# Cross-attention over states and a PReLU feed-forward on one Trainium2 core: batch 1's state scores with tokens in partitions, and the table of steps in another order

## Chip, cores and metric

The kernel runs on one core of one Trainium2 chip. The metric is the device time of one launch in microseconds; the median of the runs shown is 208.47 us (207.69 to 208.61, three runs). Profile times below are microseconds from the start of one profiled execution's span.

## What is computed

`x` holds 8 batches of 8 heads, 512 tokens and 64 values; `state` holds 32 states of 64 values for each batch and head. Tokens read states, states read tokens, and all rows go through one feed-forward layer with a PReLU:

```
scores = scale * x @ state^T             # 512 x 32 for each batch and head
xread  = softmax(scores over states) @ state
sread  = softmax(scores^T over tokens) @ x
rows   = concat(xread, sread)            # 4352 rows of 512 (8 heads x 64)
h      = rows @ w_in                     # 4352 x 2048
out    = (max(h,0) + alpha * min(h,0)) @ w_out
```

## The kernel before

The work is cut into named steps, and one table of text, `ORDER` (lines 17 to 136), lists them; the loop at line 830 executes the table word by word. A word such as `F.0.3.7` is the step's name with its arguments, often with a PSUM bank (0 to 7) or an engine (`a` ScalarE, `v` VectorE, `p` GpSimd) at its end. Each engine works through its own instructions in the order of the table, so the table is each engine's queue; what waits for what follows from the data and from the eight banks. The names that matter here:

- `wi`, `wo`, `lx`, `lst` (lines 252, 258, 199, 246): loads of a quarter of w_in or w_out, of one batch of x, of the states of batches 2 to 7. All are issued from GpSimd's queue. Only four batches of x fit, so a late `lx` also waits for the batch whose place it takes.
- `xt`, `xo`, `xo2` (lines 332, 344, 347): transposing x of batches 0 and 1 on TensorE and copying the result to `xT`. Later batches are transposed by DMA from SyncE's queue (SP), `xd` (line 326).
- Softmax over states, one of two ways. By transposition: `sc` (line 353) makes the scores with states in partitions, `sb` (463) transposes them in 32 x 32 blocks on VectorE, `smax` (475) takes maxima on VectorE, `ssh` (480) subtracts them on GpSimd, `sexp` (486) takes the exponential on ScalarE. By TensorE: `dd` (396) copies the states into a block-diagonal tile, `sd` (403) makes the scores with tokens in partitions, `hm` (419) takes maxima on VectorE, `hs` (422) subtracts them with one more matmul, `he` (432) takes the exponential on ScalarE straight from PSUM. Both ways end alike: `ssum` (490), `snorm` (495, GpSimd), `wb` (503, VectorE), which gives the weights `aT`. A batch is done by TensorE if the table has an `sd` word for it (line 376). Before, this is batch 0 alone.
- Softmax over tokens: it always uses `sc`; then `tm` (512, VectorE), `tms` and `te` (518, 521, ScalarE), `tsum` (535), a DMA transposition `tt` (539, SP), and the products and copies `rd`, `rn`, `rt`, `rdo` (546 to 576).
- The first matrix product is folded: `m` (585) multiplies the states by a quarter of w_in, `mo` (600) casts the result to f16 on ScalarE or VectorE, and `f` or `F` (637, 614), the "first products", multiply it with `aT`. `N` (649, ScalarE) rectifies, `G` (654, VectorE) finishes the PReLU.
- The second product: batch 0 plainly, `S` (671), 32 words of two matmuls of 512 columns. Batches 1 to 7, and the state rows as an eighth group, combine blocks into seven products where eight would be needed: `W` (733, GpSimd) forms sums of w_out's blocks, `A` (756, GpSimd or VectorE) sums of hidden blocks, `P` (767) the products, four matmuls of 256 columns a word, `C` and `D` (802, 807) the copies and sums to the output rows, `st` (721) the store from SP. There are four output buffers.
- `Z` (268) issues dummy matmuls in TensorE's idle head: its last argument counts pieces of 128 columns, up to four in one matmul.

Of the kernel before, what the change touches and what calls it, by code (L numbers as in the profile page):

```python
# [22 lines left out]
mo.2.0.a.1.2 mo.2.0.a.0 Z.4.5 xt.1.1.0.5 xt.1.0.0.5 xo2.1.0.v xt.1.1.1.6 xt.1.0.1.6 xo2.1.1.v
f.0.2.0.4 f.0.2.1 N.0.2.0 G.0.2 F.0.3.7 N.0.3.1 G.0.3 m.3.0.1.2 mo.3.0.a.1.3 mo.3.0.a.0 Z.5.4
m.0.1.0.3 mo.0.1.a.1.4 wo.3 mo.0.1.a.0 lx.2 sc.1.2.5.6 tm.1 f.0.0.0.4 f.0.0.1 N.0.0.2 sb.1 f.0.1.0.2
f.0.1.1 N.0.1.3 G.0.1 tms.1 m.4.0.7.1 mo.4.0.a.0.5 te.1.0 te.1.1 m.0.2.0.3 mo.0.2.v.0.6 m.1.1.7.2
mo.1.1.a.1.7 mo.4.0.a.1 mo.1.1.a.0 mo.0.2.v.1 smax.1 lx.3 ssh.p.1 W.1.0.p W.1.1.p G.0.0 F.0.5.0
F.0.7.5 m.1.3.6.3 mo.1.3.a.0.8 mo.1.3.v.1 F.0.4.2 N.0.4.0 G.0.4 N.0.7.1 G.0.7 N.0.5.3 F.0.10.1
F.0.6.7 tsum.0 F.0.8.6 N.0.8.2 G.0.8 G.0.5 m.0.3.4.3 N.0.10.0 G.0.10 mo.0.3.a.0.9 mo.0.3.a.1
S.0.1.0.2 S.0.1.1 S.0.2.0.5 S.0.2.1 m.2.1.6.4 mo.2.1.v.0.10 sexp.1 ssum.1 snorm.p.1 N.0.6.1 G.0.6  # L30
m.1.2.0.3 mo.1.2.a.1.11 mo.1.2.a.0 S.0.2.2 F.0.9.1 S.0.1.2 F.0.13.6 N.0.9.2 G.0.9 N.0.13.3 G.0.13
F.0.11.3 N.0.11.0 G.0.11 S.0.0.0.0 S.0.0.1 S.0.0.2 wb.1 F.0.15.7 F.0.12.1 S.0.1.3 N.0.15.1 G.0.15
F.0.14.6 N.0.14.2 G.0.14 S.0.2.3 S.0.1.4 S.0.0.3 N.0.12.3 G.0.12 mo.2.1.a.1 F.1.5.3 N.1.5.0 G.1.5
F.1.12.7 N.1.12.1 G.1.12 F.1.0.4 N.1.0.2 G.1.0 F.1.1.6 F.1.3.1 N.1.3.3 G.1.3 S.0.2.4 F.1.4.3 N.1.4.0
G.1.4 F.1.8.7 N.1.8.1 G.1.8 S.0.1.5 S.0.2.5 N.1.1.2 G.1.1 F.1.2.4 N.1.2.3 G.1.2 F.1.15.1 N.1.15.0
G.1.15 S.0.1.6 S.0.1.7 O.0.1.a.0 F.1.10.3 N.1.10.1 G.1.10 S.0.2.6 S.0.0.4 xd.2 sc.2.2.6.7 sb.2 tm.2
m.4.2.2.4 mo.4.2.a.0.12 smax.2 S.0.2.7 O.0.2.a.1 mo.4.2.a.1 S.0.3.0.1 F.1.9.3 N.1.9.2 G.1.9 tsum.1
F.1.11.2 N.1.11.3 G.1.11 W.0.0.p W.2.1.p W.0.1.p W.2.0.p W.3.1.p W.3.0.p A.1.0.3.0.p.0 A.1.1.3.0.p.1
tms.2 te.2.1 F.1.6.5 N.1.6.0 G.1.6 S.0.3.1 S.0.3.2 F.1.7.4 S.0.0.5 te.2.0 N.1.7.1 G.1.7 S.0.0.6
S.0.0.7 O.0.0.a.2 tt.0 tt.1 rd.0.3 rd.1.6 rn.1 A.1.1.1.0.v.0 A.1.0.3.1.v.0 m.2.3.7.2 mo.2.3.a.0.13  # L40
mo.2.3.a.1 xd.3 st.0.2 st.0.1 tt.2 S.0.3.3 F.1.13.5 ssh.p.2 sexp.2 N.1.13.2 m.3.1.0.4 mo.3.1.a.1.1
mo.3.1.a.0 A.1.1.2.0.p.0 rn.0 sc.3.2.6.7 tm.3 tms.3 lx.4 A.1.0.1.0.p.1 ssum.2 snorm.p.2 S.0.3.4
P.1.1.1.0.2 F.1.14.3 P.1.1.1.1 G.1.13 N.1.14.3 G.1.14 A.1.1.1.1.p.0 S.0.3.5 S.0.3.6 P.1.0.2.0.4
P.1.0.1.0.0 S.0.3.7 te.3.0 te.3.1 tt.3 sb.3 P.1.1.2.0.5 P.1.1.2.1 C.1.1.1.a.3 D.1.1.0 P.1.0.1.1
O.0.3.a.1 st.0.3 st.0.0 tsum.2 wb.2 m.2.2.3.1 mo.2.2.a.1.4 mo.2.2.a.0 m.3.2.6.7 mo.3.2.a.0.6 rd.2.5
lx.5 xd.4 A.1.1.2.1.p.0 P.1.0.2.1 mo.3.2.a.1 rt.0.1 rdo.0.a rn.2 smax.3 P.1.1.6.0 A.1.0.2.0.v.1
A.1.0.4.0.p.0 F.2.7.3 N.2.7.0 G.2.7 F.2.1.5 N.2.1.1 G.2.1 C.1.0.1.a.0 D.1.0.0 F.2.8.6 N.2.8.2 G.2.8
F.2.2.7 F.2.3.1 N.2.2.3 N.2.3.0 G.2.2 P.1.0.6.0 F.2.5.3 N.2.5.1 P.1.1.6.1 F.2.0.5 N.2.0.2 G.2.5
G.2.3 P.1.0.5.0.4 C.1.1.2.a F.2.11.6 N.2.11.3 G.2.11 G.2.0 A.1.0.1.1.p.1 P.1.0.5.1 F.2.9.7 P.1.1.7.0
F.2.10.3 N.2.10.1 xd.5 G.2.10 F.2.4.1 N.2.9.0 G.2.9 F.2.14.6 N.2.4.3 G.2.4 N.2.14.2 G.2.14  # L50
A.1.1.3.1.p.1 A.1.0.2.1.p.1 P.1.0.6.1 C.1.0.2.a P.1.1.7.1 ssh.p.3 sexp.3 ssum.3 P.1.1.5.0.5 F.2.13.3
rt.2.7 rdo.2.a P.1.0.7.0 C.1.1.3.a.1 P.1.0.7.1 C.1.0.3.a.2 D.1.0.1 F.2.12.1 N.2.12.1 F.2.6.6
P.1.1.5.1 G.2.12 N.2.6.0 F.2.15.7 N.2.15.3 A.1.0.4.1.p.0 G.2.6 G.2.15 N.2.13.2 G.2.13 P.1.0.4.0
P.1.0.4.1 A.2.0.1.0.p.1 C.1.0.4.a A.1.1.4.0.p.1 P.1.0.3.0 A.2.1.3.0.p.1 P.1.0.3.1 D.1.0.2 st.1.0
D.1.1.1 P.1.1.4.0 P.1.1.4.1 C.1.1.4.a st.1.3 tsum.3 rd.3.6 rn.3 sc.4.2.0.1 snorm.p.3 wb.3 m.3.3.7.3
m.4.1.4.2 mo.4.1.a.0.9 mo.3.3.a.1.0 mo.3.3.a.0 A.1.1.4.1.p.1 A.2.0.2.0.p.1 P.1.1.3.0 mo.4.1.a.1
A.2.1.1.0.v.0 A.2.0.4.0.v.0 P.2.0.1.0.6 P.2.0.1.1 P.2.0.2.0.4 C.2.0.1.a.0 F.3.5.3 N.3.5.1
A.2.0.1.1.v.1 A.2.0.2.1.p.1 F.3.1.7 N.3.1.0 tm.4 tms.4 P.2.0.6.0 P.2.0.2.1 D.2.0.0 G.3.5 F.3.3.2
N.3.3.3 G.3.3 st.1.1 P.1.1.3.1 D.1.1.2 G.3.1 st.1.2 F.3.12.4 N.3.12.2 P.2.0.6.1 C.2.0.2.a G.3.12
F.3.2.3 N.3.2.1 G.3.2 F.3.10.2 N.3.10.3 A.2.0.3.0.p.0 P.2.0.7.0 F.3.8.5 N.3.8.0 G.3.8 G.3.10 te.4.0  # L60
P.2.1.1.0.7 P.2.1.1.1 C.2.1.1.a.1 te.4.1 P.2.1.2.0.4 P.2.1.2.1 D.2.1.0 sb.4 A.2.0.3.1.p.1 F.3.9.3
P.2.0.7.1 A.2.1.1.1.p.0 N.3.9.2 sc.5.2.4.5 tm.5 A.2.1.2.0.p.0 F.3.0.2 N.3.0.1 C.2.0.3.a.2 G.3.0 lx.6
A.2.1.2.1.p.0 A.2.1.4.1.p.0 A.2.1.3.1.p.0 A.2.1.4.0.p.1 smax.4 ssh.p.4 P.2.1.6.0 P.2.1.6.1 C.2.1.2.a
F.3.13.0 N.3.13.0 tms.5 G.3.9 G.3.13 te.5.1 F.3.7.1 P.2.0.4.0 P.2.0.4.1 C.2.0.4.a te.5.0 tt.5 sb.5
P.2.1.7.0 F.3.11.2 P.2.1.7.1 N.3.7.3 C.2.1.3.a.3 P.2.0.5.0.6 P.2.0.5.1 D.2.0.1 A.3.1.3.0.p.0
A.2.0.4.1.p.1 lx.7 N.3.11.1 G.3.11 G.3.7 A.3.0.3.0.p.1 m.7.2.3.0 mo.7.2.a.1.11 mo.7.2.a.0 P.2.1.4.0
P.2.1.4.1 rt.3.5 P.2.1.5.0.4 P.2.1.5.1 sexp.4 C.2.1.4.a D.2.1.1 ssum.4 snorm.p.4 rdo.3.a F.3.6.0
N.3.6.2 G.3.6 m.5.0.2.3 mo.5.0.a.0.7 m.5.2.1.7 mo.5.2.a.0.8 P.2.1.3.0 F.3.4.5 N.3.4.0 G.3.4
mo.5.2.a.1 mo.5.0.a.1 st.2.3 P.2.0.3.0 P.2.0.3.1 F.3.15.2 N.3.15.1 D.2.0.2 st.2.0 P.2.1.3.1 D.2.1.2
st.2.1 m.4.3.0.1 mo.4.3.a.0.2 m.6.0.7.5 mo.6.0.a.0.4 m.5.1.3.6 mo.5.1.a.0.10 F.3.14.4 N.3.14.3  # L70
A.3.1.1.0.p.1 P.3.1.1.0.0 P.3.0.1.0.7 P.3.0.1.1 P.3.1.1.1 mo.5.1.a.1 mo.4.3.a.1 mo.6.0.a.1 smax.5
wb.4 ssh.p.5 G.3.15 G.3.14 P.3.1.2.0.3 A.3.0.1.0.v.0 F.4.8.6 N.4.8.2 G.4.8 tsum.4 F.4.5.1 N.4.5.0
C.3.1.1.a.3 C.3.0.1.a.0 G.4.5 P.3.1.2.1 F.4.15.2 F.4.12.4 D.3.1.0 N.4.12.1 G.4.12 F.4.10.5 N.4.10.3
G.4.10 P.3.0.2.0.6 F.4.6.1 N.4.6.2 P.3.0.2.1 F.4.2.3 N.4.2.0 G.4.6 D.3.0.0 G.4.2 F.4.7.4 N.4.7.1
G.4.7 N.4.15.3 G.4.15 A.3.0.1.1.p.1 A.3.0.2.0.p.1 P.3.0.6.0 F.4.13.5 N.4.13.2 F.4.14.1 F.4.3.6
# [787 lines left out]
```

## Time and profile before

| | us |
|---|---|
| runs shown, median | 208.47 |
| the profiled execution | 207.22 |
| its span | 205.4 |
| TensorE busy | 197.1 (96%) |
| VectorE busy | 181.6 (88%) |
| GpSimd busy | 159.6 (78%) |
| ScalarE busy | 145.2 (71%) |

The profiled execution is 1.82 longer than its span. Busy time of TensorE counts each matmul with its modelled end, so neighbours overlap; where many follow each other, the time from start to start is the better measure. The TensorE clock was granted in full (1.00) in every stage.

### The profile page before, as it was taken

Reading aid. Unit: us, or ns where it says so; the run is one execution under the profiler, and the core shown is the slowest. Engines: PE = TensorE matmul, PEld = TensorE weight load, DVE = VectorE, ACT = ScalarE, POOL = GpSimd, SP = SyncE. Lnnn points to the kernel's source line nnn. Section 1 sums busy time; section 2 is a strip of 40 time slices with the busy share of each in tenths; the row PEclk is TensorE's granted clock in tenths of the full one; section 3 lists DMA queues with packets and bytes.
Section 4 is the critical chain, followed back from the end, with each engine's and each line's share of the span. In section 5 each row is a group of like instructions: output and inputs, shape, how many; then the busy total and the mean of one; then the engine's idle time right before and its main releaser. Section 6 shows DMA issues by size and latency. Waiting matters only on the chain.

```text
span 205.4 us, 5181 instructions
## 1 busy us (share of the span) xinstructions
PE 197.1 (96%) x2023; PEld 131.4 (64%) x2023; DVE 181.6 (88%) x321; ACT 145.2 (71%) x319; POOL 159.6 (78%) x136
## 2 busy tenths in 40 slices
...
GB/s 81 195 203 209 204 206 197 185 232 54 163 163 178 66 153 58 100 103 158 194 163 3 53 123 135 3 105 102 0 0 3 111 93 3 2 131 62 69 102 156
DMA packets 39257, 23.22 MB, mean 113 GB/s; under 512 B 22320, under 2 KB 35008, under 8 KB 39232
## 3 DMA queue, kind: packets, MB, share of 16 engines
...
q1 hardware_dynamic: 26496, 14.29, 28.4%
...
HBM read 17.31 MB, written 8.91 MB: 128 GB/s over the span
## 4 chain that ended last, share of the span: by engine, by line
PE 85%; DVE 5%; DMA 5%; POOL 1%; ACT 1%; issue 1%; ACTq 0%; POOLq 0%
PE ps L793 44%; PE ps L620 24%; PE ps L675 7%; DMA xg<-in_x_dram 5%; PE ps L629 3%; PE ps L590 3%; DVE gt_all L656 3%; PE ps L553 1%; ACT neg_all L652 1%; PE ps L362 1%; DVE m_all L603 1%; POOL xg L218 1%; DVE ts L466 1%; DVE nb L514 1%; DVE mx L476 1%
## 5 line engine op out<-in xcount | busy, mean ns | idle before, releaser
L656 DVE SCALAR_TENSOR_TENSOR gt_all<-neg_all,oma_sb,ps 128x512 f16<-128x512 f32 x128 | 89.3, 738 | 3.0 <-ACT neg_all L652 2.7
L652 ACT ACTIVATE neg_all<-ps 128x512 f32<-128x512 f32 (+1 forms) x144 | 77.4, 598 | 20.0 <-PE ps L620 14.4
L620 PE MATMUL ps<-aT,m_all 128*128 128x512 f16 x250 | 66.4, 379 | 0.3 <-DVE m_all L603 0.2
L765 POOL TENSOR_TENSOR hc_all<-gt_all 128x512 f16<-128x512 f16 x43 | 49.2, 1160 | 11.4 <-DVE osb_all L810 8.7
L793 PEld LDWEIGHTS <-hc_all 128*128 128x128 f16 x480 | 46.3, 98 | 14.3 <-issue 1.1
L793 PE MATMUL ps<-wc,hc_all 128*128 128x256 f16 x360 | 47.7, 273 | 0.0
L793 PEld LDWEIGHTS <-gt_all 128*128 128x128 f16 x336 | 32.6, 98 | 8.3 <-issue 0.5
L805 ACT COPY osb_all<-ps 128x256 f32<-128x256 f32 x51 | 19.1, 383 | 25.7 <-PE ps L793 22.2
L620 PEld LDWEIGHTS <-m_all 128*128 128x128 f16 x250 | 24.0, 98 | 18.0 <-issue 2.2
L603 ACT CAST m_all<-ps 128x512 f16<-128x512 f32 x58 | 31.6, 621 | 4.3 <-PE ps L590 4.3
L765 POOL TENSOR_TENSOR hc_all<-gt_all,hc_all 128x512 f16<-128x512 f16 x22 | 25.4, 1164 | 6.3 <-DVE hc_all L765 6.1
L793 PE MATMUL ps<-w_out_sb,gt_all 128*128 128x256 f16 x224 | 29.7, 273 | 0.0
L765 POOL TENSOR_TENSOR hc_all<-hc_all,gt_all 128x512 f16<-128x512 f16 x21 | 24.3, 1164 | 3.9 <-DVE hc_all L765 3.6
L810 DVE TENSOR_TENSOR osb_all<-osb_all,ps 128x256 f32<-128x256 f32 x45 | 18.0, 413 | 7.6 <-PE ps L793 4.7
L496 POOL TENSOR_TENSOR an<-ts,r 128x1024 f16<-128x1024 f32 (+1 forms) x9 | 15.5, 1725 | 6.2 <-DVE r L493 4.0
L482 POOL TENSOR_TENSOR ts<-ts,mx 128x1024 f32<-128x1024 f32 x7 | 13.4, 1918 | 5.4 <-DVE mx L476 5.4
L675 PE MATMUL ps<-w_out_sb,gt_all 128*128 128x512 f16 x64 | 16.6, 380 | 0.1
L793 PE MATMUL ps<-w_out_sb,hc_all 128*128 128x256 f16 x120 | 16.5, 273 | 0.0
L793 PE MATMUL ps<-wc,gt_all 128*128 128x256 f16 x112 | 14.7, 273 | 0.0
L590 PE MATMUL ps<-w_in_sb,stT 64*32 64x512 f16 x256 | 11.8, 383 | 1.9 <-DMA w_in_sb<-in_moe_w_in_dram 0.9
L527 ACT ACTIVATE e<-ps,nb 128x512 f16<-128x512 f32 x16 | 11.1, 705 | 0.1
L675 PEld LDWEIGHTS <-gt_all 128*128 128x128 f16 x64 | 5.9, 98 | 7.2 <-issue 1.2
...
## 6 DMA issues: line engine op xcount, KB each, us to landing
...
w_in_sb<-in_moe_w_in_dram POOLq DMA_DIRECT2D x4, 512.0 KB, 12.0
w_out_sb<-in_moe_w_out_dram POOLq DMA_DIRECT2D x4, 512.0 KB, 13.6
...
```

What stands on the lines that cost most here:

```text
L482: engine(e).tensor_tensor(ts, ts, over_blocks(cols(softmax_tile("mx", b), j, S // N)), ALU.subtract)
L496: engine(e).tensor_tensor(blocks(cols(softmax_tile("an", b), j, S)), blocks(cols(softmax_tile("ts", b), j, S)), over_blocks(cols(softmax_t ...
L590: nc.tensor.matmul(banks[N * k : N * (k + 1), (k0, k1)[g], :], st_head(b, 2 * k + g)[64 * g : 64 * g + 64, :], w_in_sb[64 * g : 64 * g + 6 ...
L603: copier(e)(ms[b, f][:, g, :], banks[:, live["mp", b, f][g], :])
L620: nc.tensor.matmul(h.rearrange("p (r t) -> p r t", r=2), ms[b, f][:, g, 128 * j : 128 * (j + 1)], weights(b, g), start=(g == 0), stop=(g = ...
L652: nc.scalar.activation(neg, h, RELU, bias=0.0, scale=-1.0)
L656: nc.vector.scalar_tensor_tensor(gts[b, f][:, j, :], negs.pop((b, jc)), oma_sb[:, jc : jc + 1], hs.pop((b, jc)), ALU.mult, ALU.add,)
L675: nc.tensor.matmul(outs[b, q], hidden(b, jc, q), w_out_sb[:, jc, :], start=(jc == 0), stop=(jc == n_jc - 1),)
L765: engine(e).tensor_tensor(t, x, y, ALU.add if s == 1 else ALU.subtract)
L793: nc.tensor.matmul(outs[b, i, bank], rows, cols, start=(p in (1, 2, 5) and jc == 0), stop=(jc == n_jc // 2 - 1), skip_group_check=True,)
L805: copier(e)(rows_at(b, q, k)[:, 256 * half : 256 * (half + 1)], outs[b, i, "x"])
L810: nc.vector.tensor_tensor(to, to, outs[b, i, bank], ALU.add)
```

## The change

Only the table changes. The code of the steps is the same, two lines further down, since the table is two lines longer: L362 before is L364 after.

```diff
-lx0.0 lx0.1 id ni.v wi.0 oma lst stc Z.7.32 stt.2 sto.a lx.1 wi.1 dd.0.0.v wi.2 Z.7.3 xt.0.0.0.6
+lx0.0 lx0.1 id ni.v wi.0 stc oma wi.1 Z.3.22 stt.7 dd.0.1.a dd.0.0.a lx.1 lst Z.3.10 xt.0.0.0.0
```

What the new table does:

- Batch 1 has `sd`, `hm`, `hs`, `he` in place of `sb`, `smax`, `ssh`, `sexp`. Its `sc` stays, for the softmax over tokens.
- `sc.0`, `sc.1` and the token softmaxes of batches 0 and 1 come after the first products have begun (`sc.1` after twelve of them); before, `sc.0` stood ahead of all.
- The transposes of batch 1 (`xt.1`) come after six first products have begun; before, they stood ahead of the first.
- The first dummies are 22 pieces where they were 32. The second half of batch 0's `hs` comes after the first `m`; before, both halves came ahead of it.
- Engines: VectorE does four `A` (28, were 32), two `mo` (4, were 6), two `xo`, one `xo2` and one `dd` fewer, and two `C` and one `rdo` more. The `A` go to GpSimd, the others to ScalarE or from it.
- Everything behind that, to the last product, is in another order too; the number of first and second products is the same.

GpSimd's queue at its head, before: the loads of w_in, of the states (`gs_all`), of batch 1 (`xg_124`), of w_out, of batches 2 and 3, with batch 0's normalisation (L496) between them.

```order
L253 DMA w_in_sb<-in_moe_w_in_dram 128x4x512
L247 DMA gs_all<-in_state_dram 128x768
L201 DMA xg_124<-in_x_dram 128x8x256
L253 DMA w_in_sb<-in_moe_w_in_dram 128x4x512 x3
L496 TENSOR_TENSOR an_298<-ts_240,r_0_242 128x512 x2
L259 DMA w_out_sb<-in_moe_w_out_dram 128x4x512 x4
L201 DMA xg_377<-in_x_dram 128x8x256
L201 DMA xg_443<-in_x_dram 128x8x256
```

The same place after the change (lines are two higher):

```order
L255 DMA w_in_sb<-in_moe_w_in_dram 128x4x512 x2
L203 DMA xg_123<-in_x_dram 128x8x256
L249 DMA gs_all<-in_state_dram 128x768
L255 DMA w_in_sb<-in_moe_w_in_dram 128x4x512
L498 TENSOR_TENSOR an_231<-ts_225,r_0_228 128x512 x2
L261 DMA w_out_sb<-in_moe_w_out_dram 128x4x512
L255 DMA w_in_sb<-in_moe_w_in_dram 128x4x512
L261 DMA w_out_sb<-in_moe_w_out_dram 128x4x512 x3
```

The second quarter of w_in moved ahead of batch 1's x, the states behind it, and the last quarter of w_in behind the first of w_out.

ScalarE's queue at its head, before: copies of the states and of xT, batch 0's exponentials over states (L433), casts of m products (L603), batch 0's exponentials over tokens (L527), rectifiers (L652).

```order
L300 COPY stT<-ps 128x512
L398 COPY gs_all<-ps 64x8x32
L345 COPY xT_134<-ps 128x4x128
L433 ACTIVATE ts_240<-ps 128x512 x2
L603 CAST m_all<-ps 128x512 x2
L519 ACTIVATE nb_237<-nb_237 128x2
L603 CAST m_all<-ps 128x512
L317 COPY stT<-ps 128x128x6
L527 ACTIVATE e_0_307,r_0_308<-ps,nb_237 128x512 x2
L603 CAST m_all<-ps 128x512 x2
L652 ACTIVATE neg_all<-ps 128x512 x2
L603 CAST m_all<-ps 128x512 x4
```

After, from batch 0's exponentials over states (now L435):

```order
L435 ACTIVATE ts_225<-ps 128x512 x2
L605 CAST m_all<-ps 128x512 x7
L654 ACTIVATE neg_all<-ps 128x512 x6
L350 COPY xT_327<-ps 128x4x256
L654 ACTIVATE neg_all<-ps 128x512 x2
L319 COPY stT<-ps 128x128x6
L605 CAST m_all<-ps 128x512 x5
L654 ACTIVATE neg_all<-ps 128x512 x3
L435 ACTIVATE ts_490<-ps 128x512
```

The exponentials over tokens left this place; seven casts stand ahead of the first rectifier, then six rectifiers in a row.

SP's queue around batch 6's transposition, before (`xT_1697` is batch 6, `xT_1777` batch 7; `e2T` are transposed exponentials over tokens):

```order
L722 DMA out_dram<-osb_all 128x512 x3
L327 DMA_TRANSPOSE xT_1697<-xg_1350 128x16x128
L541 DMA_TRANSPOSE e2T_1699<-e_4_1293 128x8x128
L722 DMA out_dram<-osb_all 128x512
L327 DMA_TRANSPOSE xT_1777<-xg_1416 128x16x128
```

After (`xT_1744` and `xT_1943`):

```order
L724 DMA out_dram<-osb_all 128x512 x5
L329 DMA_TRANSPOSE xT_1744<-xg_1552 128x16x128
L543 DMA_TRANSPOSE e2T_1766<-e_5_1594 128x8x128
L724 DMA out_dram<-osb_all 128x512
L543 DMA_TRANSPOSE e2T_1909<-e_4_1291 128x8x128
L329 DMA_TRANSPOSE xT_1943<-xg_1617 128x16x128
```

Two transposes of exponentials now stand between the two batches, and five stores ahead of batch 6. In the table batch 6's load stood ahead of batch 4's normalisation and stands behind it now.

More of the change, by code (lines that the diff above doesn't have):

```diff
@@ L23 @@
[L23 to L75, printed above, removed]
@@ new lines @@
+N.1.0.3 G.1.0 F.1.3.7 N.1.3.0 G.1.3 N.1.11.1 S.0.2.4 G.1.11 A.1.0.3.0.p.0 A.1.1.1.0.p.0 F.1.5.2
+S.0.1.7 S.0.2.5 F.1.14.4 xd.2 sc.2.2.6.7 sb.2 tm.2 smax.2 ssh.p.2 N.1.5.2 O.0.1.a.0 G.1.5 N.1.14.3
+G.1.14 F.1.15.3 N.1.15.0 S.0.2.6 S.0.2.7 O.0.2.a.1 F.1.7.5 N.1.7.1 G.1.15 G.1.7 S.0.3.5 S.0.3.6
+S.0.0.0.1 S.0.0.1 S.0.0.2 S.0.0.3 tms.2 te.2.1 A.1.0.1.0.p.1 te.2.0 A.1.0.2.0.p.0 m.4.2.2.6
+mo.4.2.a.0.12 F.1.12.7 N.1.12.2 G.1.12 F.1.13.4 N.1.13.3 G.1.13 A.1.0.1.1.p.0 sexp.2 ssum.2
+snorm.p.2 S.0.3.7 S.0.0.4 S.0.0.5 S.0.0.6 S.0.0.7 O.0.3.a.2 mo.4.2.a.1 m.3.2.5.2 mo.3.2.a.0.13
```

177 lines of the change are left out of this document (113 added, 64 removed).

## Prediction

> **What bounds the kernel now.** I read the page first, then busy time by stage, then the chain that ended last.
>
> ```profile
> PE 197.1 (96%) x2023; PEld 131.4 (64%) x2023; DVE 181.6 (88%) x321; ACT 145.2 (71%) x319; POOL 159.6 (78%) x136
> ```
>
> TensorE (PE) is busiest, VectorE (DVE) close behind. By stage (columns: busy time of PE, weight loads, DVE, ACT, POOL):
>
> ```profile
> 10.00:20.00 10.00, 8.17 (x128) 3.70 (x128) 9.46 (x15) 9.13 (x22) 6.80 (x8) 1.00 1.30 204
> 20.00:30.00 10.00, 9.20 (x72) 3.67 (x72) 9.96 (x17) 10.00 (x22) 6.08 (x3) 1.00 1.24 207
> 30.00:40.00 10.00, 10.00 (x48) 4.54 (x47) 10.00 (x15) 7.97 (x16) 9.94 (x5) 1.00 1.28 192
> ```
>
> From 10 to 30 us DVE and ScalarE (ACT) are full while PE is not; from 30 on PE is full. The chain says the same (start, length, engine, line):
>
> ```profile
> 4.76 9.53 DMA xg<-in_x_dram
> 14.34 1.07 PE ps L340 x16
> ...
> 16.51 1.41 DVE gt_all L656 x2
> ...
> 24.41 0.67 DVE gt_all L656
> 25.12 1.89 PE ps L675 x8
> ...
> 34.19 2.16 PE ps L620 x10
> ...
> 97.61 0.61 ACT neg_all L652
> ...
> 180.04 21.85 PE ps L793 x200
> ```
>
> Batch 1's load of x lands at 14.29, its transposes stand on PE ahead of the first product, DVE carries the chain from 16.51 to 25.08, and from 25.12 PE runs almost without a gap to 201.89; the last copy and store take 3.5 more. The one exception lies around 97.61:
>
> ```profile
> 99.86 0.37 ACT L805 COPY osb_all<-ps 128x256 f32<-128x256 f32 x1 [0.90 <-DMA out_dram<-osb_all]
> ```
>
> ACT waits 0.90 us for a store to free an output buffer, and products wait for ACT. So the change can gain in two places: the head, and this gap. The rest is PE's own work, which only grows.
>
> **What is added and removed.**
>
> ```profile
> 7.48 0.94 PE L409 MATMUL ps<-gs_all,xT 128*32 128x64 f16 x64
> L423 PE MATMUL ps<-gs_all 128*128 128x512 bf16 x2 | 0.8, 376 | 0.1
> L466 DVE STREAM_TRANSPOSE ts<-ps 128x1024 f32<-128x1024 f32 x7 | 8.7, 1243 | 0.0
> L476 DVE TENSOR_REDUCE mx<-ts 128x32 f32<-128x1024 f32 x7 | 8.5, 1209 | 0.0
> L420 DVE TENSOR_REDUCE gs_all<-ps 128x16 bf16<-128x512 f32 x2 | 1.3, 687 | 0.0
> L482 POOL TENSOR_TENSOR ts<-ts,mx 128x1024 f32<-128x1024 f32 x7 | 13.4, 1918 | 5.4 <-DVE mx L476 5.4
> L603 DVE CAST m_all<-ps 128x512 f16<-128x512 f32 x6 | 4.0, 682 | 0.0
> L603 ACT CAST m_all<-ps 128x512 f16<-128x512 f32 x58 | 31.6, 621 | 4.3 <-PE ps L590 4.3
> L345 DVE COPY xT<-ps 128x512 f16<-128x512 f16 x3 | 1.2, 412 | 0.4 <-PE ps L340 0.4
> L765 POOL TENSOR_TENSOR hc_all<-gt_all 128x512 f16<-128x512 f16 x43 | 49.2, 1160 | 11.4 <-DVE osb_all L810 8.7
> L765 DVE TENSOR_TENSOR hc_all<-gt_all 128x512 f16<-128x512 f16 x13 | 5.4, 426 | 0.0
> ```
>
> PE gains 64 score matmuls (0.94, of which 0.23 was a wait) and two corrections (0.38 each, 0.22 when something follows at once): **+1.1 us**. Batch 1's whole scores for the token softmax (L362) stay, so nothing leaves PE. DVE loses the transposition (1.24) and the maxima (1.21), gains two small maxima (1.37) and gives away two casts (1.36), two copies of xT (0.82) and four hidden sums (1.70); its other copies come and go and nearly cancel: about -5. ACT takes the casts (2 x 0.62) and copies, some +3 in all (an estimate: five copies more at about the length of a cast, against three fewer short ones). GpSimd (POOL) loses one subtraction (1.92) and gains four sums (4.64): +2.7. DVE, the engine of the old head chain, is relieved; ACT and POOL are loaded.
>
> **The head, walked by the queues.** The loads come one after another:
>
> ```profile
> 3.46 0.77 POOL L253 DMA_DIRECT2D w_in_sb<-in_moe_w_in_dram  x1
> DMA to landing us min/median/max: 6.6/12.0/15.3
> 13.45 3.04 POOL L259 DMA_DIRECT2D w_out_sb<-in_moe_w_out_dram  x4
> DMA to landing us min/median/max: 11.0/13.6/16.3
> ```
>
> The first quarter of w_in lands at 3.46 + 6.6 = 10.06, the first of w_out at 13.45 + 11.0 = 24.45; between them come the states and five loads of 512 KB, so some 2.7 us each. In the new order: w_in 0 at 10.1, w_in 1 at 12.7, x of batch 1 at 15.5, states 16.5, w_in 2 at 19.3, w_out 0 at 22, w_in 3 at 24.6. The second w_in is 4 us sooner, the last 2 us later.
>
> Batch 0's second correction (L423) now stands behind the first m product (L590), which waits for w_in at 10.13; so its exponential starts at 10.8 instead of 9.73, but the weights are ready at 14.2 against 14.75, since DVE is free. The first product then runs at 14.4 instead of 15.24, as no transposes of batch 1 are ahead of it. ACT now has seven casts ahead of the first rectifier. Start to start they are short:
>
> ```profile
> 21.64 2.10 ACT L603 CAST m_all<-ps 128x512 f16<-128x512 f32 x4
> 23.54 2.65 ACT L652 ACTIVATE neg_all<-ps 128x512 f32<-128x512 f32 x5
> 29.83 2.62 DVE L656 SCALAR_TENSOR_TENSOR gt_all<-neg_all,oma_sb,ps 128x512 f16<-128x512 f32 x4
> 32.37 1.24 DVE L504 STREAM_TRANSPOSE aT<-an 128x1024 f16<-128x1024 f16 x1
> ```
>
> Four casts take 23.54 - 21.64 = 1.90 (0.48 each), rectifiers alike, prelus on DVE (32.37 - 29.83)/4 = 0.64. So the first rectifier starts at 14.6, the first prelu at 15.3 (16.51 before), and the first second product (L675) at 23.0 (25.12 before). From there PE waits again: for the two exponentials of batch 1 on ACT (banks), for casts, and for the last scores of batch 0, whose banks wait for a prelu at 30.3. By hand this gives 13 second products, 16 first products and 12 m products done at 34.1. Before, the chain from 25.12 to the end of the row 34.19 (36.35) had 13, **21** and 12 done. The missing five first products take 5 x 0.432 = 2.16 (ten matmuls in the row 34.19), so equal work is done at 34.1 + 2.16 = 36.26 against 36.35: **-0.1 us**, with the added score work already paid. For a dozen semaphore hops that my walk sums at nothing I add **+0.3**. Bounds: if PE lost nothing behind 23.0, the head would be worth -1.0; at the mean 0.62 of a cast instead of 0.48, some 30 ACT operations on the path bring +1.6 or more.
>
> **The rest.** The gap at 97.61 goes: there the store stood one product ahead of the copy that needs its buffer, now ten products and a first product (5 us) ahead: **-0.5** (0 to -0.9). POOL, followed through its queue with 1.16 a sum, ends batch 1's sum A.1.0.2.1 at 55.1, and PE wants it at 54.9: **+0.2** (0 to +1.5). The third term is batch 6's transposition:
>
> ```profile
> 80.12 0.94 POOL L201 DMA_DIRECT2D xg<-in_x_dram  x1
> 92.04 1.91 POOL L496 TENSOR_TENSOR an<-ts,r 128x1024 f16<-128x1024 f32 x1
> DMA to landing us min/median/max: 5.9/5.9/5.9
> 94.63 5.66 SPq L327 DMA_TRANSPOSE xT<-xg  x1
> DMA to landing us min/median/max: 7.7/7.7/7.7
> 111.80 0.22 PE ps L362 x16
> ```
>
> The load of batch 6 was issued at 80.12, ahead of batch 4's normalisation (92.04); now it stands behind it, so it is issued at 92 to 93 and lands 5.9 later, at 98 to 99. The transposition (7.7 to landing while a load runs beside it) ends at 106 to 107. Its user, batch 6's scores, came at 111.80 with 9 us to spare; they now stand 3.9 us of PE work earlier, at some 107. So 9 us of cover shrink to about none: **+0.5** (0 to +3). SP's queue behind it holds two transposes of exponentials, a store and batch 7's transposition, whose user comes six us of PE work later.
>
> Sum: -0.1 + 0.3 - 0.5 + 0.2 + 0.5 = **+0.4 us**. The profiled execution took 207.22 with a span of 205.4, so it would become 207.6; the runs shown have a median of 208.47, 1.25 above it, so I forecast **208.9 us**. A measurement of this kernel tells about 0.5% (1.04 us) from no change.
>
> **A rule of the skill.**
>
> ```profile
> 1.32 3.60 PE L272 MATMUL ps<-gs_all 128*128 128x512 f16 x8 [1.32 <-DVE gs_all L266]
> 6.09 0.70 PE L272 MATMUL ps<-gs_all 128*128 128x512 f16 x3
> ```
>
> The first eight dummy matmuls come 0.43 apart, those at 6.09 about half of that. The Trainium skill (TensorE: Matmul & The Clock Gate, "What's actually happening") says that the array starts at half clock and is released after about one busy window of 3.4 us. The trace agrees: 3.6 us of dummies, then full speed. The new order issues 5.5 such matmuls (2.4 us) before a short gap, so by that rule release could come a window later; doubling the transposes (0.61 for eight) and scores would bring about +0.6 us on the first exponential, most of it hidden by the wait for w_in at 10.13: an estimate of +0.2, which I leave out of the sum.
>
> **The rivals.**
> Relief of DVE pays fully (chance 0.22, faster): PE loses nothing behind 23.0 (-1.0), the old gap goes (-0.5), and no transposition is late: about -1.5 to -2, 206.7. For it speaks DVE's 9.96 of 10 in the old head; against it that ACT was as full there (10.00) and gets more.
> ACT takes DVE's place (0.20, slower): 30 operations at 0.55 to 0.62 instead of 0.48 make the head +1 to +2.5 longer than I walk it; 210.4. It decides from 0.52 each on. ACT had 9.13 and 10.00 of 10 in those stages.
> The late load of batch 6 (0.18, slower): if POOL gets to it only at 95, PE, which takes its work in order, stops at batch 6's scores for 2 to 3 us, and batch 7's follow: 211. It decides once the transposition lands later than 107.
> That the change does not do what it says (no relief, since batch 1's token scores, maxima and exponentials stay) is the forecast itself: 0.40.
>
> Chances: faster by over 0.5% 0.22, within 0.40, slower 0.38. The range takes the faster rival's centre and the late load's: 206.8 to 211.2; the likeliest case alone is 207.9 to 209.5.
>
> **What would show it.** Right: first product near 14.4, first L675 matmul near 23.0 and PE gaps until 31; DVE below 9 of 10 between 10 and 30, ACT at 9 or more; load of batch 6 behind 91 us; its scores less than 2 us behind the landing. Wrong: PE without a gap from 23 on (then faster), or a PE gap of over 1 us between 104 and 110, or sums of POOL as releasers of PE (then slower).

## The result and the profile after

The changed kernel takes **219.2 us** (median of 4 runs, 217.8 to 219.5) against 208.08 for the kernel before, measured on the same chip (207.66 to 208.61): a ratio of **1.051** (95% interval 1.047 to 1.055). The forecast was 208.9 with a range that ended at 211.2. The profiled execution took 219.0 with a span of 217.2. Code lines lie two higher than before (the hidden sums were L765 and are L767; in some experiments the table is a line shorter or longer, and they are L766).

The page's busy line for PE and the granted clock in 40 slices, of the changed kernel:

```profile
PE 202.3 (93%) x2094; PEld 133.7 (62%) x2094; DVE 187.8 (86%) x314; ACT 148.7 (68%) x325; POOL 162.3 (75%) x139
...
PE   7999999999905999999998999999999999999993
...
PEclk9999999999975899999999999999999999999999
```

PE has one hole, in the slices from 59.7 to 70.6 us, and in it the clock falls: by microsecond the granted clock is 1.00 up to 62, 0.51 in the next and 0.50 from there to 72. PE's list of waits has one entry that matters:

```profile
PE ps L622 <- DVE gt_all L658: 8.4, 1, 8.4
...
PE ps L364 <- DMA xT<-xg: 0.6, 1, 0.6
```

PE waited 8.4 us for one prelu (L658). The timeline of DVE and then of POOL around it (start, length, engine, line, operation, count):

```profile
55.65 1.18 DVE L478 TENSOR_REDUCE mx<-ts 128x32 f32<-128x1024 f32 x1
56.75 0.41 DVE L812 TENSOR_TENSOR osb_all<-osb_all,ps 128x256 f32<-128x256 f32 x1
57.08 10.00 DVE L767 TENSOR_TENSOR hc_all<-gt_all 128x512 f16<-128x512 f16 x2
```

```profile
55.26 2.27 POOL L767 TENSOR_TENSOR hc_all<-gt_all 128x512 f16<-128x512 f16 x2
57.47 0.94 POOL L203 DMA_DIRECT2D xg<-in_x_dram  x1
58.43 1.17 POOL L767 TENSOR_TENSOR hc_all<-hc_all,gt_all 128x512 f16<-128x512 f16 x1
59.53 0.91 POOL L203 DMA_DIRECT2D xg<-in_x_dram  x1
60.46 1.92 POOL L484 TENSOR_TENSOR ts<-ts,mx 128x1024 f32<-128x1024 f32 x1
62.34 1.15 POOL L767 TENSOR_TENSOR hc_all<-hc_all,gt_all 128x512 f16<-128x512 f16 x1
63.44 4.64 POOL L767 TENSOR_TENSOR hc_all<-gt_all,hc_all 128x512 f16<-128x512 f16 x4
```

Two hidden sums stand on DVE there, A.1.1.3.0 and A.1.1.3.1, and take 10.00 us together. DVE's row of that line gives minimum, median and maximum in ns:

```profile
L767 DVE TENSOR_TENSOR hc_all<-gt_all x13: 382/417/9337, 57.1 to 206.3; 128x512 f16<-128x512 f16 x13
```

The median is 0.42 us; the sum that starts at 57.74 takes 9.34 (the one ahead of it 0.74). It shows as busy, so no list of waits names it: DVE seems to work for 9 us on a sum of 0.42. All that time POOL runs without a pause. What follows on PE, from its timeline:

```profile
67.79 1.86 PE L622 MATMUL ps<-aT,m_all 128*128 128x512 f16 x4 [8.43 <-DVE gt_all L658]
...
73.01 1.03 PE L622 MATMUL ps<-aT,m_all 128*128 128x512 f16 x4
```

Four first-product matmuls take 1.86 us behind the hole (first row) and 1.03 five microseconds later (last row): PE works at half clock from 67.79 to some 72.2 (in between, rows of four matmuls of 256 columns take 1.06 instead of 0.60), which costs half of that stretch, about 2.2 us. The Trainium skill (TensorE: Matmul & The Clock Gate, "What's actually happening") has the array fall back to half clock after an idle window of some 3.4 us; the trace agrees roughly here, with half clock 2.7 us behind the end of the last matmul (59.36). So 8.4 + 2.2 + 0.6 (batch 6's scores) = 11.2 us: nearly all of the 11.4 by which the profiled 219.0 misses its forecast of 207.6 starts from one sum.

### The profile page after: what moved, and what is told of

It reads as the page before. It is cut to its first block, busy times and chain, and to the rows that moved or that the text cites. A ratio compares the mean times of both kernels' runs of the same rounds, so it can differ in the third digit from the quotient of the medians.

```text
span 217.2 us, 5320 instructions
## 1 busy us (share of the span) xinstructions
PE 202.3 (93%) x2094; PEld 133.7 (62%) x2094; DVE 187.8 (86%) x314; ACT 148.7 (68%) x325; POOL 162.3 (75%) x139
## 4 chain that ended last, share of the span: by engine, by line
PE 83%; DVE 9%; DMA 3%; ACT 1%; POOL 1%; issue 1%; DVEq 0%; POOLq 0%
PE ps L795 41%; PE ps L622 23%; PE ps L677 7%; DVE hc_all L767 5%; PE ps L592 4%; PE ps L631 3%; DMA xT<-xg 3%; DVE gt_all L658 2%; PE ps L274 1%; PE ps L555 1%; PE ps L364 1%; ACT m_all L605 1%; PE ps L342 1%; POOL xg L220 1%; POOL an L498 0%
## 5 line engine op out<-in xcount | busy, mean ns | idle before, releaser
L658 DVE SCALAR_TENSOR_TENSOR gt_all<-neg_all,oma_sb,ps 128x512 f16<-128x512 f32 x128 | 88.8, 738 | 6.9 <-ACT neg_all L654 6.7
L622 PE MATMUL ps<-aT,m_all 128*128 128x512 f16 x250 | 66.7, 386 | 8.4 <-DVE gt_all L658 8.4
L767 POOL TENSOR_TENSOR hc_all<-gt_all 128x512 f16<-128x512 f16 x43 | 49.4, 1165 | 8.6 <-PE ps L795 3.9
L622 PEld LDWEIGHTS <-m_all 128*128 128x128 f16 x250 | 23.9, 99 | 28.0 <-issue 11.3
L795 PEld LDWEIGHTS <-gt_all 128*128 128x128 f16 x336 | 32.4, 98 | 8.8 <-issue 1.2
L605 ACT CAST m_all<-ps 128x512 f16<-128x512 f32 x60 | 32.3, 611 | 5.3 <-PE ps L592 5.1
L807 ACT COPY osb_all<-ps 128x256 f32<-128x256 f32 x49 | 18.3, 385 | 23.6 <-PE ps L795 21.8
L767 POOL TENSOR_TENSOR hc_all<-gt_all,hc_all 128x512 f16<-128x512 f16 x24 | 27.6, 1165 | 9.1 <-PE ps L795 6.9
L795 PE MATMUL ps<-w_out_sb,gt_all 128*128 128x256 f16 x224 | 30.4, 273 | 0.0
L767 POOL TENSOR_TENSOR hc_all<-hc_all,gt_all 128x512 f16<-128x512 f16 x22 | 25.3, 1157 | 2.7 <-DVE hc_all L767 2.3
L812 DVE TENSOR_TENSOR osb_all<-osb_all,ps 128x256 f32<-128x256 f32 x45 | 18.2, 412 | 7.8 <-PE ps L795 5.3
L677 PE MATMUL ps<-w_out_sb,gt_all 128*128 128x512 f16 x64 | 16.0, 379 | 0.0
L767 DVE TENSOR_TENSOR hc_all<-gt_all 128x512 f16<-128x512 f16 x13 | 14.4, 1126 | 0.0
L592 PE MATMUL ps<-w_in_sb,stT 64*32 64x512 f16 x256 | 12.4, 384 | 0.3 <-DMA w_in_sb<-in_moe_w_in_dram 0.2
L484 POOL TENSOR_TENSOR ts<-ts,mx 128x1024 f32<-128x1024 f32 x6 | 11.5, 1916 | 0.0
```

The costliest lines, as they stand in the source:

```text
L484: engine(e).tensor_tensor(ts, ts, over_blocks(cols(softmax_tile("mx", b), j, S // N)), ALU.subtract)
L592: nc.tensor.matmul(banks[N * k : N * (k + 1), (k0, k1)[g], :], st_head(b, 2 * k + g)[64 * g : 64 * g + 64, :], w_in_sb[64 * g : 64 * g + 6 ...
L605: copier(e)(ms[b, f][:, g, :], banks[:, live["mp", b, f][g], :])
L622: nc.tensor.matmul(h.rearrange("p (r t) -> p r t", r=2), ms[b, f][:, g, 128 * j : 128 * (j + 1)], weights(b, g), start=(g == 0), stop=(g = ...
L658: nc.vector.scalar_tensor_tensor(gts[b, f][:, j, :], negs.pop((b, jc)), oma_sb[:, jc : jc + 1], hs.pop((b, jc)), ALU.mult, ALU.add,)
L677: nc.tensor.matmul(outs[b, q], hidden(b, jc, q), w_out_sb[:, jc, :], start=(jc == 0), stop=(jc == n_jc - 1),)
```

## The experiments

The question was what holds that sum. Theory A: any unbroken run of POOL instructions. Theory B: only a sum that meets the issue of a load, with more work queued on POOL. The rival to both: the sums were waited for, or something behind them is late whatever runs them.

**Sums on POOL.** The edit to the changed kernel:

```
- A.1.1.3.0.v.1 A.1.1.3.1.v.1
+ A.1.1.3.0.p.1 A.1.1.3.1.p.1
```

> The changed kernel, with its two sums A.1.1.3.0 and A.1.1.3.1 on GpSimd instead of VectorE. Theory (VectorE shut out by GpSimd): the 9.34 us sum is gone, PE has no wait of 8 us near 60, the clock stays at 1.0, and the time falls by 9.5 to 11 us to 208.5 to 210; GpSimd's queue gets 2 x 1.16 = 2.3 us longer. Rival (the two sums were waited for, and something behind them is late whatever runs them): PE still waits over 3 us between 57 and 70, time above 213.

Measured: 213.15 us, ratio 1.023 (1.017 to 1.030). The hole is gone, so the sums on DVE made it. But the time stopped 3 us short of what was expected, and at 213.15 it even lies where the rival had it (above 213), though without the rival's wait of over 3 us. Three costs stand in this profile: POOL, lengthened by 2.3 us, is itself late; behind that wait the clock falls (four matmuls take 1.06 at 73.32); and it fell in the head too:

```profile
71.16 0.61 PE L795 MATMUL ps<-wc,hc_all 128*128 128x256 f16 x4 [2.33 <-POOL hc_all L767]
72.27 0.61 PE L795 MATMUL ps<-wc,hc_all 128*128 128x256 f16 x4 [0.50 <-POOL hc_all L767]
...
73.32 1.06 PE L795 MATMUL ps<-w_out_sb,hc_all 128*128 128x256 f16 x4
```

```profile
11.05 0.41 PE L592 MATMUL ps<-w_in_sb,stT 64*32 64x512 f16 x8 [1.71 <-DMA w_in_sb<-in_moe_w_in_dram]
...
12.39 2.42 PE L274 MATMUL ps<-gs_all 128*128 128x512 f16 x6
```

In this execution the first quarter of w_in let PE go on at 11.05 (9.71 in the profile of the changed kernel); behind the wait six dummies took 2.42 (1.31 there) and the first product ran at 16.41 (14.37). An estimate from these rows: 2.0 us in the head, 2.8 of waits for POOL and 1.7 for half clock from 73.0 to 76.4 make 6.5 us. That is about what lies between this profiled execution (214.49) and the one of the last version below (208.66, with waits of 0.67 of its own). Both falls of the clock came behind waits shorter than the window of that rule (1.71, and 2.33 with 0.50); there the measurement decides. The four runs, 211.57 to 214.49, have mean clocks of 0.997 to 0.984, the fastest the highest and the slowest the lowest.

**Loads behind the run.** The sums stay on DVE, the loads leave:

```
- lx.4 A.1.1.2.0.p.1 lx.5 smax.3 ...
+ A.1.1.2.0.p.1 smax.3 ...
- A.1.1.3.0.v.1 A.1.1.3.1.v.1 F.2.13.2
+ A.1.1.3.0.v.1 A.1.1.3.1.v.1 lx.4 lx.5 F.2.13.2
```

> The changed kernel, with the loads of batches 4 and 5 issued behind GpSimd's run of sums instead of ahead of it and inside it; the two sums stay on VectorE. Theory A (any unbroken run of GpSimd instructions shuts VectorE out): the run is 2 x 0.95 us shorter but still some 7 us, so one of the two sums takes 6.5 to 8 us, and the time is 216 to 218. Theory B (the issue of a load shuts VectorE out, and what follows is kept waiting by it): both sums take 0.4 to 1.6 us, and the time is 208.5 to 210.

Measured: 215.78 us, ratio 1.037 (1.032 to 1.042). Its time, just under the 216 to 218 of theory A and far from the 208.5 to 210 of theory B, looks like A; the profile says the opposite:

```profile
57.19 2.04 DVE L766 TENSOR_TENSOR hc_all<-gt_all 128x512 f16<-128x512 f16 x2
```

```profile
78.19 0.63 PE L363 MATMUL ps<-xT,stT 64*32 64x256 f16 x16 [4.88 <-DMA xT<-xg]
78.75 1.89 PE L621 MATMUL ps<-aT,m_all 128*128 128x512 f16 x4
```

The two sums take 2.04 us, not 10.00, in a run of POOL's sums just as long. What is slow now is batch 4's transposition, since its load was issued at 66.52: PE waits 4.88 us and then works at half clock (1.89 for four matmuls). A total alone would have picked the wrong theory.

**One sum of the kernel before moved to DVE** (A.3.0.2.1, `.p.1` to `.v.1`):

> The kernel before, with one sum, A.3.0.2.1, moved from GpSimd to VectorE in the middle of GpSimd's run of sums from 97.70 to 109.1. Theory A: it starts near 103.8 and takes until GpSimd's last sum of the run starts, at about 106.9: 3 to 4 us instead of 0.42, with four prelus behind it late by some 3 us, so PE waits 2 to 3 us there and the time is 210 to 211.5. If VectorE waits for one GpSimd instruction at most, the sum takes up to 1.6 us and the time is 208 to 209. If VectorE isn't kept out without a load beside it, 0.42 us and 207.5 to 208.5.

Measured: 210.31 us, ratio 1.012 (1.008 to 1.016). The time is as theory A had it and the reason is not. The profiled execution took 213.10, longer than the median; the order in it still tells what happened:

```profile
105.13 4.70 DVE L656 SCALAR_TENSOR_TENSOR gt_all<-neg_all,oma_sb,ps 128x512 f16<-128x512 f32 x7
109.73 0.42 DVE L765 TENSOR_TENSOR hc_all<-hc_all,gt_all 128x512 f16<-128x512 f16 x1
```

```profile
110.21 0.61 PE L793 MATMUL ps<-wc,hc_all 128*128 128x256 f16 x4 [1.94 <-DVE hc_all L765]
```

The sum stood behind seven prelus, ran with POOL idle in 0.42 us, and PE waited 1.94 us for it. It never met POOL's run, so it says nothing of the hold: a badly placed experiment.

**The wait by itself.** POOL runs a sum, then more; DVE has sums of two SBUF operands that wait for the first. Shortened:

```
pool(0)
load()                    # in some of the cases
for k in range(n): pool(k + 1)
two(0); two(1)            # on VectorE
```

> Leaves out the whole computation, and writes two blocks of the output only: it measures the disputed wait by itself. GpSimd runs a sum of two 128x512 operands in SBUF, then n more of them back to back (n = 0, 1, 2, 4, 8), while VectorE has two such sums that wait for the first. Theory A (shut out until GpSimd pauses): the first VectorE sum takes 0.42 us at n = 0, some 1.2 at n = 1, and about 1.16 more for each further one, to 8 or 9 at n = 8. One instruction at most: no more than 1.6 at any n. Behind a load in place of a sum: 0.42 under A if only sums shut VectorE out, 0.9 to 1.4 if the issue of a load does too. With a pause in the run, which ScalarE sets behind three sums: A gives a first sum of some 2.3 us that ends in the pause. A multiply-add with one operand in SBUF and one in PSUM beside four sums: 0.7 us, not held. The other way round, a GpSimd sum behind nine VectorE sums in a row: 1.2 us if each VectorE sum lets go, about 4 if the row holds.

Two cases tell the theories apart: POOL's nine sums in a row, and a load with four sums behind it (DVE's rows, then POOL's):

```profile
31.79 2.65 DVE L70 TENSOR_TENSOR v<-p,b 128x512 f16<-128x512 f16 x2 [6.48 <-POOL p L59]
...
45.34 0.76 DVE L70 TENSOR_TENSOR v<-p,b 128x512 f16<-128x512 f16 x2 [10.91 <-POOL p L59]
50.61 5.60 DVE L70 TENSOR_TENSOR v<-p,b 128x512 f16<-128x512 f16 x2 [4.51 <-POOL p L59]
```

```profile
50.52 0.92 POOL L64 DMA_DIRECT2D xg<-in_x_dram  x1
51.45 4.46 POOL L59 TENSOR_TENSOR p<-a,b 128x512 f16<-128x512 f16 x4
```

Beside nine sums each DVE sum takes some 1.36 us: it waits for the POOL sum that runs, gets its turn, and the next POOL sum takes 1.33 instead of 1.15. Beside a load with nothing ready behind it, two DVE sums take 0.76: no wait. Beside a load with four sums behind it, the two take 5.60: the first 0.43, and the second is held until the last POOL sum is over (51.45 + 4.46 = 55.91; DVE ends at 56.21). A multiply-add of DVE with one operand in PSUM takes 0.75 beside five sums, and two sums of POOL among nine of DVE take 1.15 and 1.33: neither is held. **Theory A falls, B stands** (the third measurement by itself, below, narrows it). The Trainium skill (SBUF — State Buffer, "Who interferes with whom") says that a VectorE instruction with two SBUF inputs contends with a GpSimd instruction that reads SBUF, that the ports which they share are an exclusive lock, and that issue order decides who blocks. The nine sums agree with that, each engine waiting for one instruction of the other (1.36 and 1.33 us); the hold of 5.26 us behind a load goes beyond it, and there the measurement decides.

**Out of the load's way.** In the changed kernel, the two sums one reduction earlier on DVE:

```
- ... lx.5 smax.3 ssh.p.3 ... D.1.0.0 A.1.1.3.0.v.1 A.1.1.3.1.v.1 F.2.13.2
+ ... lx.5 A.1.1.3.0.v.1 A.1.1.3.1.v.1 smax.3 ssh.p.3 ... D.1.0.0 F.2.13.2
```

> The changed kernel, with its two sums A.1.1.3.0 and A.1.1.3.1 on VectorE one reduction (1.18 us) earlier in its queue, so that they start beside GpSimd's sums at 55.3 to 57.5 and not in the issue of batch 4's load at 57.47. Theory B (a VectorE sum that starts while GpSimd issues a load, with GpSimd sums queued behind it, is held until that run ends): both sums take 0.4 to 1.4 us, no wait of PE near 60, time 208 to 210. If any neighbourhood of GpSimd's run holds them, one takes over 5 us again and the time is 215 or more.

Measured: **209.87 us**, ratio 1.008 (1.004 to 1.012). Starting 1.55 us sooner, beside sums instead of a load, takes 9.3 us off. The two sums take 2.33 us. PE's row:

```profile
59.37 0.60 PE L795 MATMUL ps<-wc,hc_all 128*128 128x256 f16 x4 [1.86 <-DVE osb_all L812]
```

What is left is a wait of 1.86 us: the sums, still slowed by turns, now stand ahead of the addition (L812) that frees PE's bank.

**A load under a DVE sum of the kernel before:**

```
- A.2.0.4.1.p.1 lx.7     + A.2.0.4.1.p.1
- ssh.p.5 G.3.15         + ssh.p.5 lx.7 G.3.15
```

> The kernel before, with one edit: batch 7's load is issued behind batch 5's subtraction, at 97.17 instead of 89.98, so that VectorE's sum A.3.0.1.0 (97.54) starts in its issue, ahead of GpSimd's run of ten sums. Theory B: that sum takes 4 to 11 us instead of 0.42, until GpSimd's run ends or stops for want of PE; PE waits 2 to 8 us behind it, and the time is 211 to 217. If a load's issue alone counts, the sum takes 0.9 to 1.3 us and the time is 207.5 to 209. If nothing of it holds, 0.42 us.

Measured: 207.38 us, ratio 0.996 (0.993 to 0.9996). The same kernel again:

> e6_before_load_at_sum once more, with more runs, since its interval (0.9931 to 0.9996) all but touched 1: if the later load of batch 7 is a gain, the ratio is 0.995 to 0.998 again and its interval stays below 1; if that was the spread of the runs, the interval holds 1.

Measured: 207.86 us, ratio 0.997 (0.994 to 1.0004): the interval holds 1. No hold, and no gain that the runs can tell from no change. The sum started at 97.75, inside the issue (97.33 to 98.27), with ten POOL sums behind, and took 0.42. Against theory B as stated, then. One thing differs in the order of the program: POOL's first sum behind this load needs two prelus of DVE that end at 97.84, inside the issue, while the one behind the load in the changed kernel needs nothing so late. The third measurement by itself, below, tests that.

**Batch 6's load ahead as well** (`lx.6` from behind `wb.4` to behind `tsum.3`, on top of the earlier sums):

> e5_sums_earlier, and batch 6's load ahead of batch 2's last five sums on GpSimd. Theory: PE's wait of 0.59 us for batch 6's transposition goes, so the time is 0.3 to 0.9 us under that of e5_sums_earlier. Rival (that wait was covered by what PE loses later): no difference.

Measured: 209.69 us, ratio 1.007 (1.003 to 1.010), against 209.87: no difference. Without the hold PE has no wait for batch 6 in either.

**By itself, twice more.** First the length of POOL's run, the place of the load, who issues it, and the kind of DVE's operation:

> Leaves out the whole computation, and writes two blocks of the output only. GpSimd runs a first sum, issues a load, and then runs n sums (n = 1, 2, 8); VectorE has two sums that wait for GpSimd's first. Theory B: the first takes 0.43 us, the second is held until the last of the n ends, so 1.9, 3.0 and 9.6 us or so. Then the load stands one and two sums later, with three VectorE sums: those that start beside sums take up to 1.4 us each, the one that starts in the load's issue is held for the four sums behind it, some 5 us. With the transfer issued by SyncE instead: 1.4 us each, no hold. With one operand in SBUF and one in PSUM: 0.75 us each, no hold. With a pause in GpSimd's run behind two sums: the held sum ends in the pause, some 3 us.

DVE's rows: eight sums behind the load; the load one sum later; the transfer issued by SP; one operand in PSUM; a pause in POOL's run.

```profile
17.65 10.02 DVE L71 TENSOR_TENSOR v<-p,b 128x512 f16<-128x512 f16 x2 [4.14 <-POOL p L60]
...
31.82 7.99 DVE L71 TENSOR_TENSOR v<-p,b 128x512 f16<-128x512 f16 x3 [4.14 <-POOL p L60]
...
57.32 2.64 DVE L71 TENSOR_TENSOR v<-p,b 128x512 f16<-128x512 f16 x2 [5.37 <-POOL p L60]
...
66.44 2.06 DVE L122 SCALAR_TENSOR_TENSOR v<-p,one,bank 128x512 f16<-128x512 f16 x3 [6.48 <-POOL p L60]
...
77.34 3.40 DVE L71 TENSOR_TENSOR v<-p,b 128x512 f16<-128x512 f16 x2 [8.83 <-POOL p L60]
```

As B has it in every row: with eight sums behind the load the second is held 9.68 us of the 10.02; with the load one sum later (and alike with two) the sum that starts 0.26 us into its issue is held, 5.43 of the 7.99; issued by SP, or with one operand in PSUM, nothing is held; a pause lets it in. (The case of one sum ran beside the set-up and shows nothing.)

Then what catches a sum, and what lets it go:

> Leaves out the whole computation, and writes two blocks of the output only. GpSimd: a sum, the issue of a load, four sums. VectorE has one sum, which starts about 0.1, 0.35, 0.5 and 0.85 us into the issue. Theory B as it stands: all but the first are held for some 5 us; if only a sum that stands right behind another one is held, all take 0.42 us. Then the first sum behind the load waits for VectorE's work ahead of its sum (as in e6_before_load_at_sum, where nothing was held): 0.42 us there. Then the third of five sums behind the load waits for the second, and the fourth of six for the second (as the last one of the changed kernel's run waited for an earlier one): if such a wait is what lets VectorE in, the held sum ends some 2.5 and 3.7 us behind the load's issue instead of 5.8 and 7. Last, two loads with a sum between them and four sums behind: held over both, some 7.5 us.

DVE's rows: a lone sum 0.76 us into the issue, behind an operation that reads PSUM; the same, but POOL's first sum behind the load waits for that operation; five sums of which the third waits for the second; two loads.

```profile
36.05 4.93 DVE L71 TENSOR_TENSOR v<-p,b 128x512 f16<-128x512 f16 x1
...
44.85 0.42 DVE L71 TENSOR_TENSOR v<-p,b 128x512 f16<-128x512 f16 x1
...
52.73 3.40 DVE L71 TENSOR_TENSOR v<-p,b 128x512 f16<-128x512 f16 x2 [7.46 <-POOL p L60]
...
75.66 2.91 DVE L71 TENSOR_TENSOR v<-p,b 128x512 f16<-128x512 f16 x2 [4.15 <-POOL p L60]
```

A lone sum 0.36, 0.49 or 0.76 us into the issue is held (5.33, 5.20, 4.93), one 0.09 into it is not (0.43). If POOL's first sum behind the load needs the result of that operation, which comes at 44.94, inside the issue (44.09 to 45.00), DVE's sum isn't held either (0.42): that is the case of the load moved under DVE's sum above. POOL started that sum at 45.03, so the rows show the need and no time lost by it. A sum of POOL that needs what the one just ahead of it writes ends the hold (3.05 in the third row); one that needs a result of two sums ahead does not (7.46 in a run of six). Two loads went against the expectation: DVE's sum ends as the second load is issued, after 2.57, not 7.5.

**Loads behind the subtraction.** With that, the smallest cure: in the changed kernel the two loads step back behind batch 3's subtraction on POOL, and the sums stay.

```
- lx.4 A.1.1.2.0.p.1 lx.5 smax.3 ssh.p.3
+ A.1.1.2.0.p.1 smax.3 ssh.p.3 lx.4 lx.5
```

> The changed kernel, with the loads of batches 4 and 5 behind GpSimd's subtraction for batch 3 (issued at some 60.6 and 61.5 instead of 57.47 and 59.53); the two sums stay where the change put them on VectorE, behind the addition that PE waits for. Theory B (only a VectorE sum that meets the issue of a load, with sums queued behind it, is held to the end of GpSimd's run): the sums take 0.74 and 1.4 us, PE waits neither 8.4 us near 60 nor the 1.86 us of e5_sums_earlier, and the time is 207.5 to 208.6. If any load inside that run holds a sum that runs ahead of it: 215 or more. If the later load makes batch 4's transposition late, as in e2_loads_behind: a wait of PE for xT near 75 and 209 to 212.

Measured: **209.07 us** (208.66 to 209.67, 12 runs), ratio 1.004 (1.002 to 1.007). That is a little above the 207.5 to 208.6 expected, but of 11 us lost by the change, 10 come back by moving two instructions of 0.9 us. Its rows of DVE, POOL and PE:

```profile
56.84 2.03 DVE L767 TENSOR_TENSOR hc_all<-gt_all 128x512 f16<-128x512 f16 x2
```

```profile
57.25 1.33 POOL L767 TENSOR_TENSOR hc_all<-hc_all,gt_all 128x512 f16<-128x512 f16 x1
58.55 2.09 POOL L484 TENSOR_TENSOR ts<-ts,mx 128x1024 f32<-128x1024 f32 x1
```

```profile
59.58 1.25 PE L622 MATMUL ps<-aT,m_all 128*128 128x512 f16 x4 [0.45 <-DVE gt_all L658]
...
73.17 0.41 PE L364 MATMUL ps<-xT,stT 64*32 64x256 f16 x16 [0.22 <-DMA xT<-xg]
```

The sums take turns with POOL (2.03; POOL's 1.33 and 2.09 are longer than its usual 1.15 and 1.92), and PE loses 0.45 + 0.22. No version here beats the kernel before by more than its measurement can tell.

## Why the prediction was wrong, step by step

**The step that failed** is the price of DVE's hidden sums. The prediction says that DVE "gives away ... four hidden sums (1.70)": a count times the mean of their row, 426 ns, wherever a sum stands. The four are a balance. By the two tables 17 sums leave DVE and 13 come to it from POOL, and the two of A.1.1.3 are among the 13. The new table puts them where POOL issues batch 4's load, and there one costs 9.34 us; PE waits 8.4 for it and loses 2.2 more through the clock. No term, bound or rival covered it: the text followed POOL's queue for when PE wants a sum, never for what runs on POOL while DVE executes one. The profile of before held a hint. The extremes of its rows:

```profile
L765 DVE TENSOR_TENSOR hc_all<-gt_all x13: 384/419/540, 48.3 to 193.1; 128x512 f16<-128x512 f16 x13
```

```profile
L765 POOL TENSOR_TENSOR hc_all<-gt_all x43: 1146/1157/1272, 44.4 to 188.5; 128x512 f16<-128x512 f16 x43
```

The 540 and the 1272 are pairs that met (DVE at 48.34 beside POOL's 46.66 to 48.59; POOL at 97.70 beside DVE's 97.54): the two engines wait for each other. And nearly all of that kernel's DVE sums ran while POOL was idle, none in the issue of a load. The mean hid both.

**The other steps**, read in the changed kernel up to 57 us and in the last version above:

- The head came out as walked: first product 14.37 (14.4), first rectifier 14.78 (14.6), first prelu 15.41 (15.3), first second product 23.28 (23.0). At equal work: the first-product matmuls (L622, L620) up to 34.00 in the changed kernel and up to 36.35 before are counted by the busy time of the line alone (PE with its count, weight loads, clock)

```profile
0.00:34.00 34.00, 6.58 (x25) 2.13 (x26) 1.00 1.18 184
```

```profile
0.00:36.35 36.35, 9.08 (x36) 3.44 (x36) 1.00 1.19 184
```

  and with the six of the first block in each (L643, L641) 31 and 42, at 13 second and 12 m products both. The missing 11 take 11 x 0.216 = 2.4, so 36.4 against the forecast 36.26 and 36.35 before.
- The number of the head fits, its reason does not. "From there PE waits again", for ACT above all, did not happen: PE's list has no wait between the one at 21.62 and the hole, and "PE without a gap from 23 on", named as a sign of being wrong and then faster, came without being faster. ACT did not take DVE's place, and DVE was not below 9 of 10 in both stretches as foretold: 8.32 from 10 to 20 us, but 9.96 in the next (columns PE, weight loads, DVE, ACT, POOL):

```profile
20.00:30.00 10.00, 9.67 (x138) 3.51 (x129) 9.96 (x16) 9.82 (x21) 3.87 (x2) 1.00 1.24 207
```

```profile
21.62 0.42 PE L411 MATMUL ps<-gs_all,xT 128*32 128x64 f16 x32 [0.24 <-DVE gt_all L658]
...
25.45 0.60 PE L622 MATMUL ps<-aT,m_all 128*128 128x512 f16 x2
25.99 0.41 PE L592 MATMUL ps<-w_in_sb,stT 64*32 64x512 f16 x8
```

  What pays the earlier start back is PE's own work that now stands behind it: the first second product is 1.84 us earlier, with 22 first-product matmuls done (20 before), but with three m products, both score blocks of batch 0 and both corrections of batch 1 still to do. From start to start these are 3 x 0.28 + 2 x 0.23 + 2 x 0.22 = 1.74, less 0.43 for the two matmuls more. The remaining 0.5 goes at the changes to short groups (two matmuls take 0.54 ahead of an m product, 0.43 elsewhere): an estimate from these rows. That the walk met the number with another reason is luck in part.
- The gap at 97.61 went (-0.5): behind 73.17 the last version has no wait of PE at all.
- "POOL just late" (+0.2): no wait of PE for it with the sums on DVE. There was little room: with only two more sums on POOL, PE waits 2.33 + 0.50 for it.
- Batch 6's transposition (+0.5): 0.59 measured, but only in the stretched kernel; without the hold its load is issued at 92.97, as forecast, and its scores wait for nothing. The term was 0.5 too high.
- The clock: the eight transposes of a block of batch 0 show when full speed began in the changed kernel,

```profile
5.63 1.04 PE L342 MATMUL ps<-ident,xg 128*128 128x128 f16 x8
...
7.53 0.61 PE L342 MATMUL ps<-ident,xg 128*128 128x128 f16 x8
```

  that is, around 7 us, while before the same eight took 0.61 at 5.65 already. It came later, as the rule would have it, and w_in's landing hid it, as said: the first product was on time. What the estimate of +0.2 did not cover is a later fall: in the execution with the sums on POOL w_in came late, the clock fell behind that wait, and the first product was 2 us late.

With the hold out of the way the kernel takes 209.07 where 208.9 was forecast (a profiled 208.66 for 207.6); against the kernel before, measured beside it at 207.99, that is +1.08 where +0.4 was forecast. That the parts nearly fit does not mend the forecast: the change as made contains the hold.

**Open:** why the second load in the changed kernel (59.53) did not let the sum in and the one in the measurement by itself did, and what let it in at 66.8, one sum ahead of the end of POOL's run. POOL's last sum there (66.76) needs one that ran at 62.34, but in the third measurement by itself such a need did not end the hold (7.46). Nor do the runs show what inside the engines gives way; the conditions above are what is shown.
